# A linear-attention and feed-forward kernel: its small matmuls on four quarters of the TensorE array

## The chip, the cores and the metric

The program runs on one core of one Trainium2 chip, in one launch. The metric is the device time of the execution in microseconds; a profiled execution gives in addition the trace from which the rows below are taken.

## What is computed

Four batches of 768 tokens with 8 heads of 48 channels go through a gated linear attention, and its output through a feed-forward layer with an ELU:

```python
for t in range(S):
    state = alpha[:, :, t, :, None] * state + np.einsum('bhd,bhe->bhde', k[:, :, t], v[:, :, t])
    y[:, :, t] = np.einsum('bhd,bhde->bhe', q[:, :, t], state)
x = y.transpose(0, 2, 1, 3).reshape(3072, 384)
h = x @ w_in                              # 384 -> 2048
g = np.where(h > 0, h, np.exp(np.minimum(h, 0)) - 1)
out = g @ w_out                           # 2048 -> 384
```

All inputs and the output are float32.

## The kernel before

**Attention by windows.** The tokens are cut into 24 windows `i` of 128 tokens, six to a batch (`NW`), each of two chunks of 64 tokens. Heads go in pairs: `n` is the pair (0 to 3), `a` the head within it; on the 128 partitions head `a` has rows 64a to 64a + 47. Each piece of a window is a token of the program, a function of some lines:

- `L`, `LV`, `V0` (L155, L173, L180): loads of k, q, alpha (tile `qka`), of v (tile `vs`), and of a copy of v of which only the first 64 tokens are filled, the rest zero (tile `v0`).
- `SC` (L189): running product P of alpha. `LN`, `EX` (L198, L203): its inverse R. `KA`, `KB`, `KC` (L211, L216, L221): k scaled by it. `SQ` (L235): q scaled, into tile `st`; from window 6 on (`EARLY`) each head's half of `st` apart, and `ZS` (L242) clears the other half. `PC` (L225) sums P for a check of ranges.
- `TA`, `TB` (L266): scaled k transposed in blocks of 32 by 32 on VectorE, into tile `kn`, eight instructions each.
- `S` (L293): the scores of a chunk's 64 tokens among themselves; per chunk, pair and head one fp32 matmul of 64 weight columns and 64 moving columns, 16 a window. `MK` (L301): the mask, from PSUM into the other half of `st`.
- `U` (L315): what the window adds to the state, `kn` against v, 48 columns by 48; `x = 0` from the first 64 tokens (with `v0`), `x = 1` from all 128, 8 matmuls each; a batch's last window has `x = 0` only. Both lie in one PSUM bank, tile `u`. `UA`, `UB`, `UC` (L331, L333, L362, L364): the states from it.
- `Y` (L380): the output of the window, one matmul per chunk, pair and head, over state and scores at once (128 rows), 16 a window. `XH`, `XL`, `XD` (L433, L434, L456, L460, L467): it is split into an upper and a lower part and put into the layout of x.

In windows before `EARLY` the matmuls of S and U have other shapes: S has 48 rows, on the rows of its head, and writes to the same half of the partitions (tiles (0,0) and (1,1) of four of 64 by 64); U has weights 64 columns wide, with 128 rows for `x = 1` and 64 rows for `x = 0`. The early Y has two matmuls one after the other on the same tile, one for the state and one for the scores, for each chunk, pair and head.

**Feed-forward by blocks.** A block `b` has 256 tokens, and eight steps `j`. A step is `A` (L577): 18 matmuls of 128 by 128 by 256 columns into tile `h`; `RA`, `RB` on ScalarE (L585, L590), `RC` on VectorE (L595), `GH` on ScalarE (L601) and `GL` on VectorE (L614), which make the ELU and split it into `gh` and `gl`; and `O` (L628): 12 matmuls of 384 columns into the two banks of `o`. `Z` (L636, L639) stores a block. `CA`, `CB`, `LC` check ranges of the weights.

**What sets the order.** The list `START`, written out by hand, gives the order of the first part. From step n = 25 on (n = 8b + j) the function `steady` writes the order: each step has A(n), its five elementwise operations, and O of step n - 2; every window's tokens are put at fixed steps, one window in four steps. `at(n, start, names)` puts the tokens of window i at step 4i + start. Y of a window, U of the next and S of the one behind it stand in one step, ahead of its A. Each engine runs its instructions in this order. All PSUM tiles come from one pool of eight banks.

In the trace and below an fp32 matmul stands as two passes, each with a weight load; the matmuls of A and O are one pass each.

Of the kernel before, what the change touches and what calls it, by code (L numbers as in the profile page):

```python
# [8 lines left out]
F32 = mybir.dt.float32  # L9
# [55 lines left out]
GH.2.1 LV.11 SQ.9 ZS.9 RA.2.4 XL.7 RB.2.4 GL.2.2 UC.8 SC.10 XD.7 LN.10 EX.10 GL.2.1 S.9 PC.9 TA.9 KA.10 A.2.5  # L65
RA.2.5 O.2.1 RB.2.5 O.2.2 RC.2.4 A.3.0 UA.8 A.2.7 RC.2.5 GH.2.6 GH.2.4 RA.3.0 RB.3.0 O.2.3 MK.9 RA.2.7 S.8
GH.2.5 GL.2.4 O.2.4 TB.9 GL.2.6 GL.2.5 UB.6 RB.2.7 LV.9 V0.9 MK.8 L.11 KB.10 KC.10 SQ.10 ZS.10 RC.3.0 RC.2.7
O.2.5 GH.3.0 TB.10 TA.10 GL.3.0 GH.2.7 GL.2.7 V0.10 O.2.6
"""

@with_exitstack
def gla_elu_ffn(ctx: ExitStack, tc: tile.TileContext, qka, vv, vn, wgt, out):
    nc = tc.nc
# [7 lines left out]
    psa = main.enter_context(tc.tile_pool(name="psa", bufs=8, space=bass.MemoryType.PSUM))  # L81
# [55 lines left out]
    win = [{} for _ in range(NWIN)]  # L137
# [38 lines left out]

    @tok
    def V0(i):
        if i >= EARLY:
            nc.sync.dma_start(out=v0[i % 2][0:64], in_=vv[i, 0:64, HD:2 * HD])  # L180

    @tok
# [54 lines left out]

    @tok
    def ZS(i):
        if i >= EARLY:  # L240
            for a in range(2):
                nc.gpsimd.memset(win[i]["st"][64 - 64 * a:128 - 64 * a, a], 0.0)  # L242

# [54 lines left out]
    def MK(i):  # L298
        d = win[i]
        for o, a in ([(slice(0, 128), 1)] if i < EARLY else [(slice(64, 128), 0), (slice(0, 64), 1)]):  # L300
            nc.vector.tensor_tensor(  # L301
                out=d["st"][o, a].rearrange("p n (c t) -> p c n t", c=2), in0=d["sc"][o],
                in1=mask[o].unsqueeze(1).unsqueeze(1).broadcast_to([o.stop - o.start, 2, NP, C]), op=ALU.mult)

    @tok
    def U(i):
        d = win[i]
        u = d["u"] = psa.tile([128, 2, NP, D], F32, name="u", tag="pa")
        m = 64 if i < EARLY else D
        for x in ((1, 0) if i % NW < NW - 1 else (0,)):  # L310
            r = slice(0, C) if x == 0 and i < EARLY else slice(0, 128)
            v = d["vn"] if x or i < EARLY else v0[i % 2].rearrange("p (h e) -> p h e", e=D)
            for n in range(NP):
                for a in range(2):
                    nc.tensor.matmul(u[64 * a:64 * a + m, x, n, :], lhsT=d["kn"][r, n, a, 0:m],  # L315
                                     rhs=v[r, 2 * n + a, :],
                                     start=(x == int(i % NW < NW - 1) and n == 0), stop=True, skip_group_check=True)


    def rows(i):  # L320
        return [slice(0, 128)] if i < EARLY else [slice(0, D), slice(64, 64 + D)]

    def state(i, r, c):
        a = r.start // 64
        return lhs(i, c, a)[r, 0:NP * D].rearrange("p (n e) -> p n e", e=D)


    def diff(i, out, r, x):
        u = win[i]["u"][r, x]
        if i % NW == 0 or i in UPE:  # L330
            nc.scalar.mul(out=out, in_=u, mul=-1.0)  # L331
        else:
            nc.vector.tensor_tensor(out=out, in0=state(i, r, 0), in1=u, op=ALU.subtract)  # L333

    @tok
    def UP(i):
        for x in range(2 if i % NW < NW - 1 else 1):
            for a in range(2 if i >= EARLY else 1):
                r = slice(64 * a, 64 * a + D) if i >= EARLY else slice(0, 128)
                nc.tensor.matmul(win[i]["u"][r, x], lhsT=minus[:, r].bitcast(F32), rhs=lhs(i, 0, a)[:, 0:NP * D],  # L340
                                 start=False, stop=True, skip_group_check=True)

    @tok
    def UA(i):
        for r in rows(i):
# [328 lines left out]
    start = [t.split(".") for t in START.split()]  # L674
# [10 lines left out]
def steady(n0=25):  # L685


    p, late = [], [divmod(n, NJ) for n in range(n0 - 2, n0)]

    def at(n, start, names, end=NWIN):  # L690
        if (n - start) % 4 == 0 and (n - start) // 4 < end:
            p.extend((x, (n - start) // 4) for x in names)

    def second(b, j):
        p.append(("O", b, j))
        if j == NJ - 1:
            p.append(("Z", b))

    for n in range(n0, NBLK * NJ):
        b, j = divmod(n, NJ)  # L700
        at(n, -18, ("V0",))
        at(n, -22, ("L", "LV"))
        at(n, -7, ("Y",))
        at(n, -11, ("U",))
        at(n, -15, ("S",))
        if n == 4 * NWIN - 4:
            p.append(("VP",))
        p.extend((x, b, j) for x in ("A", "RA"))
        at(n, -17, ("LN",))
        p.append(("RB", b, j))  # L710
        at(n, -17, ("EX", "KA", "KB", "ZS", "ZV"))
# [12 lines left out]
        at(n, -7, ("XL", "XD"))
        at(n, -11, ("UA", "UB", "UC"))
        at(n, -13, ("MK",))
        at(n, -14, ("PC",))
# [188 lines left out]
```

## Time and profile before

| | us |
|---|---|
| median of 3 runs | 523.03 (522.64 to 526.26) |
| profiled execution | 524.14 |
| its span, first to last instruction | 522.4 |
| TensorE busy | 509.1 |
| VectorE busy | 396.4 |
| ScalarE busy | 298.0 |
| GpSimd busy | 133.0 |

The span is the time between the first and the last instruction in the trace; the profiled execution has some time around it. Busy time of an engine is the time in which at least one of its instructions runs. Matmuls are pipelined, so their rows overlap: how long one costs is read from the distance of starts, not from its duration.

### The profile page before, as it was taken

The page shows a single profiled execution, that of the slowest core. Times are in us where ns is not written, and L with a number is a line of the kernel's source. Part 1 is how long each engine was busy: PE and PEld are TensorE (multiplying, and loading weights), DVE is VectorE, ACT ScalarE, POOL GpSimd, SP SyncE. Part 2 cuts the span into 40 slices and gives each one's busy share as a digit, 9 for nine tenths or more (in the row PEclk, how much of TensorE's full clock was granted, in tenths as well). Part 3 has the DMA queues.
Part 4 walks back from the last instruction along what each step waited for, and adds up shares of the span by engine and source line. Part 5 has one row for each costly group of instructions (what it writes and reads, how often), then busy time and mean ns, then how long its engine had stood idle before and what let it go on. Part 6 is the DMA issues. An engine that isn't in the chain of part 4 may idle for free.

```text
span 522.4 us, 13159 instructions
## 1 busy us (share of the span) xinstructions
PE 509.1 (97%) x5398; PEld 490.4 (94%) x5406; DVE 396.4 (76%) x781; ACT 298.0 (57%) x682; POOL 133.0 (25%) x137
## 2 busy tenths in 40 slices
PE   6899999999999999999999999999999999999996
PEld 3688899999999999999999999999999999999996
DVE  7889999899998777776877887786887877334431
ACT  3337576455652657657656657557657656654442
POOL 2214552434230034044044044043043140000000
PEclk8889999999999999999999999999999999999999
DMA  8992930415122234344344254254154131110001
GB/s 301 412 375 55 414 118 1 159 54 189 66 77 69 84 115 137 100 130 136 89 141 137 74 157 137 62 167 136 57 174 136 36 101 42 48 52 9 30 3 35
DMA packets 23843, 62.90 MB, mean 120 GB/s; under 512 B 3168, under 2 KB 11232, under 8 KB 23776
## 3 DMA queue, kind: packets, MB, share of 16 engines
q1 hardware_dynamic: 23488, 61.60, 36.1%
q8 instruction: 44, 0.72, 0.6%
q10 hardware_dynamic: 288, 0.39, 0.2%
q14 instruction: 23, 0.19, 0.1%
HBM read 55.30 MB, written 4.72 MB: 115 GB/s over the span
## 4 chain that ended last, share of the span: by engine, by line
PE 96%; DVE 2%; DMA 1%; issue 1%; SPq 0%; ACT 0%; DVEq 0%
PE h L577 40%; PE o L628 39%; PE sc L293 5%; PE y L380 4%; PE u L315 3%; PE y L375 2%; DMA qka<-in_qka_dram 1%; PE tp L256 1%; PE wp L109 1%; PE y L419 1%; DVE st L232 0%; PE yl L375 0%; DVE wm L515 0%; DVE P L189 0%; SPq L159 0%
## 5 line engine op out<-in xcount | busy, mean ns | idle before, releaser
L577 PE MATMUL h<-xt,w 128*128 128x256 f32 x1728 | 222.5, 283 | 0.0
L577 PEld LDWEIGHTS h<-xt,w 128*128 128x128 f32 x1728 | 213.7, 188 | 2.0
L628 PE MATMUL o<-w,gh 128*128 128x384 f32 x768 | 198.6, 340 | 0.0
L628 PEld LDWEIGHTS o<-w,gh 128*128 128x128 f32 x768 | 135.6, 188 | 0.4
L628 PE MATMUL o<-w,gl 128*128 128x384 f32 x384 | 129.8, 338 | 0.0
L585 ACT ACTIVATE r<-h 128x512 f32<-128x512 f32 x96 | 57.4, 598 | 110.8 <-PE h L577 102.9
L595 DVE SCALAR_TENSOR_TENSOR h<-r,h 128x512 f32<-128x512 f32 x96 | 66.2, 694 | 66.8 <-ACT r L590 66.4
L601 ACT CAST gh<-h 128x512 fp32r<-128x512 f32 x96 | 56.0, 586 | 66.2 <-DVE h L595 54.9
L614 DVE TENSOR_TENSOR gl<-h,gh 128x512 fp32r<-128x512 f32 x96 | 65.7, 686 | 32.2 <-ACT gh L601 31.3
L266 DVE STREAM_TRANSPOSE kn<-qka 32x128 f32<-32x128 f32 x288 | 87.0, 302 | 3.8
L235 POOL TENSOR_TENSOR st<-qka,P 64x512 f32<-64x512 f32 x30 | 36.3, 1209 | 200.4 <-PE h L577 109.0
L628 PEld LDWEIGHTS o<-w,gl 128*128 128x128 f32 x384 | 72.2, 188 | 0.0
L590 ACT ACTIVATE r<-r 128x512 f32<-128x512 f32 x96 | 60.3, 631 | 2.2
L189 DVE TENSOR_TENSOR_SCAN P<-qka,first 128x516 f32<-128x516 f32 x24 | 30.5, 1274 | 2.4 <-DMA qka<-in_qka_dram 1.8
L211 POOL TENSOR_TENSOR qka<-qka,R 128x512 f32<-128x512 f32 x18 | 23.5, 1306 | 27.8 <-ACT R L203 20.8
L301 DVE TENSOR_TENSOR st<-sc,mask 64x512 f32<-64x512 f32 (+1 forms) x42 | 28.9, 688 | 1.9 <-PE sc L293 0.8
L216 POOL TENSOR_TENSOR R<-P,R 128x512 f32<-128x512 f32 x20 | 25.6, 1278 | 16.0 <-DVE qka L211 12.8
L293 PE MATMUL sc<-st,qka 128*64 128x64 f32 (+1 forms) x768 | 29.2, 232 | 0.0
L293 PEld LDWEIGHTS sc<-st,qka 128*64 128x64 f32 (+1 forms) x768 | 26.4, 146 | 2.2 <-issue 1.8
L380 PEld LDWEIGHTS y<-st,vs 128*64 128x64 f32 x576 | 18.2, 138 | 4.5 <-issue 4.3
L533 ACT ACTIVATE ck<-ck,lim 128x384 f32<-128x384 f32 x32 | 21.0, 655 | 1.0
L380 PE MATMUL y<-st,vs 128*64 128x64 f32 x576 | 20.7, 225 | 0.0
(87 smaller groups left out, 424.4 us busy)
## 6 DMA issues: line engine op xcount, KB each, us to landing
qka<-in_qka_dram SPq DMA_DIRECT2D x22, 770.0 KB, 5.6
raw<-in_wgt_dram SPq DMA_DIRECT2D x16, 768.0 KB, 11.4
ck<-in_wgt_dram SPq DMA_DIRECT2D x32, 384.0 KB, 3.5
vs<-in_vv_dram SPq DMA_DIRECT2D x36, 192.0 KB, 5.4
out_dram<-ot SPq DMA_DIRECT2D x22, 192.0 KB, 2.7
vs<-in_vv_dram SPq DMA_DIRECT2D x6, 384.0 KB, 10.2
xt<-y SPq DMA_DIRECT2D x40, 48.0 KB, 3.1
v<-in_vv_dram SPq DMA_DIRECT2D x18, 96.0 KB, 3.1
```

The lines of the kernel that those rows point to most:

```text
L189: nc.vector.tensor_tensor_scan(out=P.rearrange("p n w -> p (n w)"), data0=t[:, 2 * NP * W:], data1=first.rearrange("p n w -> p (n w)"), in ...
L235: eng(SQV, i).tensor_tensor(out=st[r, a], in0=d["q"][r], in1=pw(i)[r], op=ALU.mult)
L266: nc.vector.transpose(out=kn[32 * t:32 * t + 32, :, 32 * g:32 * g + 32], in_=d["kt"][32 * g:32 * g + 32, :, 32 * t:32 * t + 32])
L293: nc.tensor.matmul(sc[o, c, n, :], lhsT=d["kt"][r, n, cs], rhs=d["st"][r, 0 if i < EARLY else a, n, cs], start=(c == 0 and n == 0), stop=T ...
L380: nc.tensor.matmul(out[64 * a:64 * a + m], lhsT=lhs(i, c, a)[:, n * D:n * D + m], rhs=d["st"][:, a, n, c * C:(c + 1) * C], start=start, st ...
L577: nc.tensor.matmul(h[:, f, :], lhsT=t[:, wi, ws], rhs=x[:, c, xi, :], start=(f == 0 and k == 0), stop=(k == 8), skip_group_check=True)
L585: nc.scalar.activation(out=r, in_=d["h"], func=AF.Relu, scale=-1.0)
L590: nc.scalar.activation(out=d["r"], in_=d["r"], func=AF.Exp, scale=-1.0)
L595: nc.vector.scalar_tensor_tensor(out=d["h"], in0=d["r"], scalar=-1.0, in1=d["h"], op0=ALU.add, op1=ALU.max)
L601: nc.scalar.copy(out=gh, in_=d["h"])
L614: nc.vector.tensor_tensor(out=gl, in0=d["h"], in1=d["gh"].bitcast(F32), op=ALU.subtract)
L628: nc.tensor.matmul(o[:, 0:DM], lhsT=gt[:, f, ms], rhs=t[:, wi, f * DM:f * DM + DM], start=(j == 0 and f == 0 and k == 0), stop=(j == NJ - ...
```

## The change

From window 10 on (`QUAD`) U has another form, from window 11 on S has.

- **U4** replaces the two halves of U, all tokens and first 64 tokens, by the first and the second 64 tokens: `x` is the half of the tokens, and with it the 64 rows of the array; `a` is the head, and with it the 64 columns. A matmul has 64 rows, 64 weight columns (all of `kn`'s, with padding) and 48 moving columns. Each half x has a PSUM bank of its own (tiles `q`). A batch's last window has x = 0 only.
- **S4** has for each head `a` and chunk `c` the 48 rows of the head and writes to the partitions of the chunk. The scores lie behind U's columns in the two banks that U4 of the window before got, by head.
- Both loops run over `QUADS`, so that four matmuls that follow each other are on four quarters of the array.
- `MK` becomes four operations of 64 x 256, in two parts. `UB` starts from what `UA` made, since u's second part is now of the second tokens alone, and is there in a batch's first window too; `UC` has one form.
- `V0` ends with window 9, `ZS` with window 10.
- `steady` puts tokens at other places: XH, XL, XD ahead of A; SC ahead of RA; LN and EX behind GH and one step earlier; KA and KB one step earlier; KC at the end of its step, also one earlier; the transposes in pieces (T.0 and T.1, T.2, T.3) over three steps instead of one; MK in two pieces; UA ahead of GH; PC one step later. The check of the weights moves by two steps.

```diff
+    QUADS = ((0, 0), (1, 1), (0, 1), (1, 0))
+    def S4(i):
+        d = win[i]
+        d["s4"] = [t[:, NP * D:NP * (D + C)].rearrange("p (n t) -> p n t", n=NP) for t in win[i - 1]["q4"]]
+        for n in range(NP):
+            for a, c in QUADS:
+                r, cs = slice(64 * a, 64 * a + D), slice(c * C, (c + 1) * C)
+                nc.tensor.matmul(d["s4"][a][64 * c:64 * c + 64, n, :], lhsT=d["kt"][r, n, cs], rhs=d["st"][r, a, n, cs],
+                                 start=(n == 0 and a == 1 and i % NW == 0), stop=True, skip_group_check=True)
...
+        if i > QUAD:
+            for a, c in QUADS[2 * part:2 * part + 2] if part < 2 else QUADS:
+                o, r = slice(64 * c, 64 * c + 64), slice(64 - 64 * a, 128 - 64 * a)
+                nc.vector.tensor_tensor(
+                    out=d["st"][r, a, :, c * C:(c + 1) * C], in0=d["s4"][a][o],
+                    in1=mask[o].unsqueeze(1).broadcast_to([64, NP, C]), op=ALU.mult)
+            return
...
+    def U4(i):
+        d = win[i]
+        d["q4"] = banks(i)
+        d["u"] = [t[:, 0:NP * D].rearrange("p (n e) -> p n e", n=NP) for t in d["q4"]]
+        for n in range(NP):
+            for x, a in QUADS if i % NW < NW - 1 else QUADS[::2]:
+                r = slice(64 * x, 64 * x + 64)
+                nc.tensor.matmul(d["u"][x][64 * a:64 * a + 64, n, :], lhsT=d["kn"][r, n, a, :],
+                                 rhs=d["vn"][r, 2 * n + a, :], start=(n == 0), stop=True, skip_group_check=True)
...
-        if i >= EARLY:
+        if EARLY <= i < QUAD:
             nc.sync.dma_start(out=v0[i % 2][0:64], in_=vv[i, 0:64, HD:2 * HD])
...
-        at(n, -16, ("TA", "TB"))
...
+        at(n, -14, "T.2")
+        at(n, -13, "MK.1", "PC")
+        at(n, -13, "T.3")
+        at(n, -17, "KC")
+        at(n, -16, "T.0", "T.1")
```

TensorE, a step of the steady part with a window in it, before (`o`: O's tiles, `y`, `u`, `sc`: those of Y, U and S, `h`: A's):

```order
L628 MATMUL o<-w_756,gh 128x384 x2
L628 MATMUL o<-w_756,gl 128x384
L380 MATMUL y<-st,vs_106 64x64 x16
L315 MATMUL u<-vs_107,kn 48x48 x8
L315 MATMUL u<-v_113,kn 48x48 x8
L293 MATMUL sc<-st,qka 64x64 x16
L577 MATMUL h<-xt,w_909 128x256 x18
```

and such a step of the changed kernel (`q`: the shared banks):

```order
L675 MATMUL o<-w_756,gl 128x384
L427 MATMUL y<-st,vs_108 64x64 x16
L345 MATMUL q<-vs_105,kn 64x48 x16
L302 MATMUL q<-st,qka 64x64 x16
L624 MATMUL h<-xt,w_909 128x256 x18
L675 MATMUL o<-w_756,gh 128x384 x2
```

The place and the number of matmuls are the same; the outputs of U are 64 partitions and no longer 48, and S and U write the same tiles.

VectorE in the steady part, before, from RC and GL (`h`, `gl`) of the step ahead of MK (`st<-sc`) to those of the step behind the transposes (`kn`):

```order
L595 SCALAR_TENSOR_TENSOR h<-r,h 128x512
L614 TENSOR_TENSOR gl<-h,gh 128x512
L301 TENSOR_TENSOR st<-sc,mask 64x2x4x64 x2
L595 SCALAR_TENSOR_TENSOR h<-r,h 128x512
L221 SCALAR_TENSOR_TENSOR qka<-R,qka 128x512
L614 TENSOR_TENSOR gl<-h,gh 128x512
L266 STREAM_TRANSPOSE kn<-qka 32x4x32 x16
L595 SCALAR_TENSOR_TENSOR h<-r,h 128x512
L614 TENSOR_TENSOR gl<-h,gh 128x512
```

and the same stretch of the changed kernel:

```order
L269 STREAM_TRANSPOSE kn<-qka 32x4x32 x4
L642 SCALAR_TENSOR_TENSOR h<-r,h 128x512
L329 TENSOR_TENSOR st<-q,mask 64x4x64 x2
L661 TENSOR_TENSOR gl<-h,gh 128x512
L329 TENSOR_TENSOR st<-q,mask 64x4x64 x2
L269 STREAM_TRANSPOSE kn<-qka 32x4x32 x4
L224 SCALAR_TENSOR_TENSOR qka<-R,qka 128x512
L642 SCALAR_TENSOR_TENSOR h<-r,h 128x512
L661 TENSOR_TENSOR gl<-h,gh 128x512
L269 STREAM_TRANSPOSE kn<-qka 32x4x32 x8
```

The sixteen transposes that stood in one run are now three runs in three steps, the masks stand on both sides of a GL, and KC (`qka<-R,qka`) has gone from ahead of a GL to the end of the step before.

## Rows read from the trace of the kernel before

**Rows 1.** The page: span, TensorE's busy time, the chain that ended last by engine.

```profile
span 522.4 us, 13159 instructions
...
PE 509.1 (97%) x5398; PEld 490.4 (94%) x5406; DVE 396.4 (76%) x781; ACT 298.0 (57%) x682; POOL 133.0 (25%) x137
...
PE 96%; DVE 2%; DMA 1%; issue 1%; SPq 0%; ACT 0%; DVEq 0%
```

**Rows 2.** Busy time by stretch (instructions), then clock, DMA: one of twelve, and their sum.

```profile
300.00:320.00 20.00, 20.00 (x218) 19.68 (x218) 16.47 (x37) 12.37 (x31) 5.90 (x6) 1.00 0.45 130
...
sum 240.00, PE 240.00 PEld 236.14 DVE 189.39 ACT 151.98 POOL 71.78; mean PE 20.00 PEld 19.68 DVE 15.78 ACT 12.66 POOL 5.98
```

**Rows 3.** Timeline, TensorE, a full window's step: start, length, engine, line, shapes, count.

```profile
307.26 1.15 PE L380 MATMUL y<-st,vs 128*64 128x64 f32 x32
308.24 0.53 PE L315 MATMUL u<-vs,kn 128*48 128x48 f32 x16
308.60 0.53 PE L315 MATMUL u<-v,kn 128*48 128x48 f32 x16
308.96 1.12 PE L293 MATMUL sc<-st,qka 128*64 128x64 f32 x32
310.00 2.38 PE L577 MATMUL h<-xt,w 128*128 128x256 f32 x18
312.22 0.52 PE L628 MATMUL o<-w,gh 128*128 128x384 f32 x2
...
314.34 2.30 PE L577 MATMUL h<-xt,w 128*128 128x256 f32 x18
316.48 0.52 PE L628 MATMUL o<-w,gh 128*128 128x384 f32 x2
```

**Rows 4.** Timelines of TensorE up to chosen moments: the small matmuls of some windows.

```profile
308.96 0.23 PE L293 MATMUL sc<-st,qka 128*64 128x64 f32 x1
...
308.96 0.24 PE L293 MATMUL sc<-st,qka 128*64 128x64 f32 x2
...
72.69 0.91 PE L293 MATMUL sc<-st,qka 48*64 48x64 f32 x24
...
72.69 1.15 PE L293 MATMUL sc<-st,qka 48*64 48x64 f32 x32
...
90.94 0.61 PE L315 MATMUL u<-vs,kn 64*64 64x48 f32 x14
...
90.94 0.67 PE L315 MATMUL u<-vs,kn 64*64 64x48 f32 x16
...
40.38 1.27 PE L315 MATMUL u<-vs,kn 128*64 128x48 f32 x32
...
98.11 2.13 PE L375 MATMUL y<-st,vs 48*64 48x64 f32 x64
```

**Rows 5.** Timeline, TensorE, as in rows 3: last windows of batches.

```profile
208.80 0.53 PE L315 MATMUL u<-v,kn 128*48 128x48 f32 x16
...
210.20 2.38 PE L577 MATMUL h<-xt,w 128*128 128x256 f32 x18
...
447.60 0.53 PE L315 MATMUL u<-v,kn 128*48 128x48 f32 x16
448.06 2.38 PE L577 MATMUL h<-xt,w 128*128 128x256 f32 x18
```

**Rows 6.** VectorE's groups, 200 to 430 us: count, busy us, mean ns, idle ahead.

```profile
L266 DVE STREAM_TRANSPOSE kn<-qka 32x128 f32<-32x128 f32 x183 | 55.3, 302 | 2.3
L595 DVE SCALAR_TENSOR_TENSOR h<-r,h 128x512 f32<-128x512 f32 x47 | 32.7, 696 | 26.0 <-ACT r L590 25.8
...
L301 DVE TENSOR_TENSOR st<-sc,mask 64x512 f32<-64x512 f32 x24 | 16.5, 689 | 0.7
...
L221 DVE SCALAR_TENSOR_TENSOR qka<-R,qka 128x512 f32<-128x512 f32 x12 | 8.2, 684 | 0.0
L333 DVE TENSOR_TENSOR vs<-vs,u 48x192 f32<-48x192 f32 x18 | 6.2, 347 | 0.1
```

More of the change, by code (lines that the diff above doesn't have):

```diff
@@ L32 @@
 WARM = 12
+QUAD = 10
 WLV, KAV, KBV, SQV = (0, 1, 2, 7, 9, 11, 15), (0, 1, 3, 4, 5, 9), (0, 1, 4, 7), (0, 1, 2, 6, 7, 10)
@@ L67 @@
 GH.2.5 GL.2.4 O.2.4 TB.9 GL.2.6 GL.2.5 UB.6 RB.2.7 LV.9 V0.9 MK.8 L.11 KB.10 KC.10 SQ.10 ZS.10 RC.3.0 RC.2.7
-O.2.5 GH.3.0 TB.10 TA.10 GL.3.0 GH.2.7 GL.2.7 V0.10 O.2.6
+O.2.5 GH.3.0 TB.10 TA.10 GL.3.0 GH.2.7 GL.2.7 O.2.6
 """
@@ L239, in ZS @@
     def ZS(i):
-        if i >= EARLY:
+        if EARLY <= i <= QUAD:
             for a in range(2):
@@ L269, in TA, with T @@
     @tok
+    def T(i, g):
+        blocks(i, (g,))
+    @tok
     def TA(i):
@@ L281, in KN, with banks @@
         nc.scalar.copy(out=kn, in_=d["tp"].rearrange("p n (a x) -> p n a x", a=2))
+    def banks(i):
+        return [psa.tile([128, 512], F32, name="q", tag="pa") for _ in range(2)]
+    QUADS = ((0, 0), (1, 1), (0, 1), (1, 0))
[7 more added lines that the diff above has]
+                                 start=(n == 0 and a == 1 and i % NW == 0), stop=True, skip_group_check=True)
     @tok
@@ L285, in S @@
         d = win[i]
+        if i > QUAD:
+            return S4(i)
         sc = d["sc"] = psa.tile([128, 2, NP, C], F32, name="sc", tag="pa")
@@ L297, in MK @@
     @tok
-    def MK(i):
+    def MK(i, part=2):
         d = win[i]
+        if i <= QUAD and part == 0:
+            return
+        if i > QUAD:
+            for a, c in QUADS[2 * part:2 * part + 2] if part < 2 else QUADS:
[3 more added lines that the diff above has]
+                    in1=mask[o].unsqueeze(1).broadcast_to([64, NP, C]), op=ALU.mult)
+            return
         for o, a in ([(slice(0, 128), 1)] if i < EARLY else [(slice(64, 128), 0), (slice(0, 64), 1)]):
@@ L307, in U @@
         d = win[i]
-        u = d["u"] = psa.tile([128, 2, NP, D], F32, name="u", tag="pa")
+        if i >= QUAD:
+            return U4(i)
+        u = psa.tile([128, 2, NP, D], F32, name="u", tag="pa")
+        d["u"] = [u[:, 0], u[:, 1]]
         m = 64 if i < EARLY else D
@@ L314, in U @@
                 for a in range(2):
-                    nc.tensor.matmul(u[64 * a:64 * a + m, x, n, :], lhsT=d["kn"][r, n, a, 0:m],
+                    nc.tensor.matmul(d["u"][x][64 * a:64 * a + m, n, :], lhsT=d["kn"][r, n, a, 0:m],
                                      rhs=v[r, 2 * n + a, :],
@@ L328, in diff @@
     def diff(i, out, r, x):
-        u = win[i]["u"][r, x]
-        if i % NW == 0 or i in UPE:
+        u = win[i]["u"][x][r]
+        half = i >= QUAD and x == 1
+        if (i % NW == 0 or i in UPE) and not half:
             nc.scalar.mul(out=out, in_=u, mul=-1.0)
         else:
-            nc.vector.tensor_tensor(out=out, in0=state(i, r, 0), in1=u, op=ALU.subtract)
+            nc.vector.tensor_tensor(out=out, in0=state(i, r, int(half)), in1=u, op=ALU.subtract)
     @tok
@@ L339, in UP @@
                 r = slice(64 * a, 64 * a + D) if i >= EARLY else slice(0, 128)
-                nc.tensor.matmul(win[i]["u"][r, x], lhsT=minus[:, r].bitcast(F32), rhs=lhs(i, 0, a)[:, 0:NP * D],
+                nc.tensor.matmul(win[i]["u"][x][r], lhsT=minus[:, r].bitcast(F32), rhs=lhs(i, 0, a)[:, 0:NP * D],
                                  start=False, stop=True, skip_group_check=True)
@@ L350, in UB @@
     def UB(i):
-        if i % NW < NW - 1 and i % NW and i not in UPE:
+        if i % NW < NW - 1 and (i >= QUAD or i % NW and i not in UPE):
             for r in rows(i):
-                diff(i, win[i]["u"][r, 1], r, 1)
+                diff(i, win[i]["u"][1][r], r, 1)
     @tok
@@ L360, in UC @@
             for r in rows(i + 1):
-                if i % NW and i not in UPE:
-                    nc.vector.tensor_tensor(out=state(i + 1, r, 0), in0=d["u"][r, 1], in1=pe[r], op=ALU.mult)
+                if i >= QUAD or i % NW and i not in UPE:
+                    nc.vector.tensor_tensor(out=state(i + 1, r, 0), in0=d["u"][1][r], in1=pe[r], op=ALU.mult)
                 else:
-                    nc.vector.scalar_tensor_tensor(out=state(i + 1, r, 0), in0=d["u"][r, 1], scalar=-1.0,
+                    nc.vector.scalar_tensor_tensor(out=state(i + 1, r, 0), in0=d["u"][1][r], scalar=-1.0,
                                                    in1=pe[r], op0=ALU.mult, op1=ALU.mult)
@@ L685, in steady, with at @@
 def steady(n0=25):
+    LEFT = dict(T=11)
     p, late = [], [divmod(n, NJ) for n in range(n0 - 2, n0)]
-    def at(n, start, names, end=NWIN):
-        if (n - start) % 4 == 0 and (n - start) // 4 < end:
-            p.extend((x, (n - start) // 4) for x in names)
+    def at(n, start, *names):
+        i, r = divmod(n - start, 4)
+        if r == 0 and LEFT.get(names[0].split(".")[0], 0) <= i < NWIN:
+            for x in names:
+                x, *k = x.split(".")
+                p.append((x, i, *map(int, k)))
     def second(b, j):
@@ L700, in steady @@
         b, j = divmod(n, NJ)
[L701 to L705, printed above, removed]
+        at(n, -22, "L", "LV")
+        at(n, -7, "Y")
+        at(n, -11, "U")
+        at(n, -15, "S")
         if n == 4 * NWIN - 4:
             p.append(("VP",))
[L708 to L711, printed above, removed]
+        at(n, -7, "XH", "XL", "XD")
+        p.append(("A", b, j))
+        at(n, -18, "SC")
+        p.extend((x, b, j) for x in ("RA", "RB"))
         p.append(("RC", b, j))
-        at(n, -16, ("KC",))
-        at(n, -18, ("SC", "SQ"))
+        at(n, -18, "SQ")
+        at(n, -11, "UA")
+        at(n, -13, "MK.0")
         p.append(("GH", b, j))
-        at(n, -7, ("XH",))
-        for start, h in ((21, 0), (24, 1)):
+        at(n, -18, "LN", "EX", "KA", "KB", "ZV")
+        for start, h in ((23, 0), (24, 1)):
             h += (n - start) // 4 * 2
@@ L722, in steady @@
         p.append(("GL", b, j))
-        at(n, -16, ("TA", "TB"))
[L724 to L727, printed above, removed]
+        at(n, -11, "UB", "UC")
+        at(n, -14, "T.2")
[3 more added lines that the diff above has]
+        at(n, -16, "T.0", "T.1")
         if n == 4 * NWIN - 7:
```

## The prediction

> **What bounds the kernel now.** The first view to read is the page's head: of a span of 522.4 us TensorE is busy 509.1, and the chain of work that ended last is 96% TensorE [rows 1]. A busy TensorE need not be a full one, so the second view is the busy time by stretch: over twelve stretches of 20 us from 200 to 440 us TensorE has 240.00 of 240.00, VectorE 189.39, ScalarE 151.98 and GpSimd 71.78, at a granted clock of 1.00, which is the 2.4 GHz level [rows 2]. The third view is TensorE's timeline over one step with a window in it [rows 3]: 12 matmuls of O end, then 32 passes of Y, 32 of U and 32 of S start one behind the other, then the 18 of A, and no row names a releaser. From the starts: Y takes 308.24 - 307.26 = 0.98 us, U 0.36 + 0.36, S 1.04, A 2.22. So in the steady part a microsecond taken from TensorE's own work is a microsecond of the span, as long as nobody becomes late. (An fp32 matmul of the program is two passes, two records, in the trace.)
>
> **How the passes lie.** Two passes of S start together, within 0.01 us: the first alone has a row of 0.23 us, both together one of 0.24 [rows 4]. They are the two column halves of the array (heads a = 0 and 1). The next pair comes a weight load later: 24 passes that ran up to one moment span 0.91 us, all 32 span 1.15, so four pairs cost 0.24, **0.06 a pair**. For U with weights 64 wide and 48 moving columns 14 passes span 0.61 and 16 span 0.67, again 0.06 [rows 4]; with weights 48 wide, as U has now, 16 passes take 0.36, 0.045 a pair [rows 3]. So the width of the weights sets the round of a tile, and two tiles share a round. That the halves run as queues of their own is seen in the early Y at 98.11: there two matmuls, four passes, stand in a row for the same tile before the other tile's four. Were they started strictly in order, four passes would cost three rounds and a bit, about 0.19 us; 64 passes span 2.13, so about (2.13 - 0.24)/63 = 0.030 each, 0.12 for four [rows 4]. The engine does look past passes that wait for their tile.
>
> **The change, part by part.** What matters is that S and U now use four tiles of 64 by 64, in the order (0,0), (1,1), (0,1), (1,0). The number of matmuls stays: 16 of S, 16 of U (8 in a batch's last window). If four tiles share a round as two do, 32 passes are 8 rounds of 0.06 = 0.48 us.
>
> U4 and S4 stand together in 13 steps (U of windows 10 to 22, S of 11 to 23), and U of window 23 alone in one. Windows 11, 17 and 23 are last windows.
> - Before, a full step has U + S = 310.00 - 308.24 = 1.76 us [rows 3]; a step with a last window's U has 210.20 - 208.80 = 1.40; U of window 23 with the way to A 448.06 - 447.60 = 0.46 [rows 5].
> - After: U4 8 rounds, 0.48. The weights are now the whole 64 columns, so the round is 0.06 and not 0.045. A last window's U4 has only tokens' half 0, two tiles: 16 passes, 8 rounds, 0.48 too, where it had 0.36.
> - S4 0.48, and what S has beyond its rounds stays: 1.04 - 16 x 0.06 = 0.08.
> - Y keeps 128 rows, U4 has 64, so the array changes its shape between them, which it did not before. The early U changes from 128 to 64 rows in its middle: its 32 passes span 1.27 where S of the same width without that change spans 1.15 [rows 4]. I take 0.12. Bounds: nothing, and 0.19, which is what leaving S costs now (A takes 2.22 behind S, 312.22 - 310.00, and 2.14 behind O, 316.48 - 314.34 [rows 3]: 0.08, and not more than 0.11 at S's end).
>
> Sum: a full step 1.76 - (0.48 + 0.48 + 0.08 + 0.12) = 0.60, eleven times 6.60; a last window's step 1.40 - 1.16 = 0.24, twice 0.48; window 23's U 0.46 - (0.48 + 0.10 + 0.12) = -0.24. **Together 6.84 us.** With r for the round of four tiles the sum is 18.36 - 192 r: 16 rounds in each of eleven steps and S's 8 in two.
>
> What costs nothing, and under what cover:
> - **Masks.** MK is four operations of 64 x 256 for two of 64 x 512 at 0.689 us. Between the 192-column row (0.347) and that one [rows 6] a 256-column one lies at about 0.43: 4 x 0.43 - 1.38 = +0.34 us per window on VectorE; the bounds, 0.35 and 0.69, make it 0 to 1.4. UB in windows 12 and 18 adds two operations of about 0.35.
> - **New order on VectorE.** The 16 transposes (0.302 each, 4.8 us in a run) are split 8 + 4 + 4 over three steps. The fullest step is then RC and GL (0.70 each), four masks 1.72, four transposes 1.21, KC 0.68: 5.0 us against a TensorE step of 2.12 + 2.14 = 4.26 [rows 3, 6]. The step behind has RC, GL and eight transposes, 3.8; the one with Y lasts over 6 us on TensorE. GL(n) is wanted by O(n), which stands behind A(n+2): two steps of 4.26 from A(n)'s end to that place, against 3.5 or so for RA, RB, RC, GH and GL. So 0.7 us of lateness is covered, about 5 us are. Cover gone, it would cost 0.7 in each of 13 windows.
> - **SC** goes ahead of RA to RC in its step: 1.2 us on VectorE, behind which RC and GL queue. Its input is loaded four steps earlier.
> - **XH, XL and XD** go ahead of A. XH waits for Y; behind it on ScalarE is RA, which needs A, 1.2 us of U and S and 2.2 of A later. XD's DMAs leave SP earlier.
> - **GpSimd** loses two memsets a window, SP one DMA; neither is waited for here.
> - **Two shared banks** are held from U(i) to MK(i+1), two steps, where before one bank was held so long and one for a step. Y, U4 and A take theirs over from h tiles whose GL was waited for by an O already passed, so no new stall.
>
> **A rule against the change.** The smallest mean spacing that any row shows is U's 0.36/16 = 0.0225 us a pass [rows 3]; pairs start closer, but never pair after pair. S4 and U4 want 0.06/4 = 0.015. The Trainium skill, "TensorEngine Tiling (Array Packing)", section Instruction Overhead, says that a matmul has some 60 cycles of overhead and that no tiling factor should be taken from a dimension that is already small; here 48 and 64 columns move. At 2.4 GHz that would be 25 ns a pass, r = 0.10 and a loss of 0.8 us, an estimate from that page. By that rule U's passes could not come at 0.0225; the trace has them below it.
>
> **Rivals.**
> 1. *Four tiles share the round, stretched.* If each further tile adds up to its start offset, r = 0.06 + 2 x 0.01 = 0.08: gain 3.0, 520.0 us. For it: four tiles have more weights and columns to fetch in a round than two, and no row shows that. Against it: the early S on 48 rows and the S on 128 have the same round, so what is fetched did not set it [rows 3, 4].
> 2. *The issue is the limit*, at U's 0.0225 a pass, r = 0.09: gain 1.1, 521.9 us. For it: nothing faster is in the trace. Against it: U's round fits the width of its weights (0.045 at 48, 0.06 at 64), so U is not limited by issue. This is what the page's rule above would do here.
> 3. *Two at a time; it becomes slower.* Tiles (0,0) and (1,0) write the same half of PSUM's partitions, into two banks, and no row of before has two row groups at once on one column group: the early S has only the diagonal. If they take turns, r = 0.12 and the sum is 18.36 - 23.04 = -4.7, 527.7 us. It decides from r = 18.36/192 = 0.096 on.
> 4. *VectorE late.* The 0.7 us of its fullest step reaches O each time: 13 x 0.7 = 9 us lost, 525.3 us. Against it: VectorE has 189.39 of 240 [rows 2], about 83% after, and two steps of slack.
>
> **The numbers.** The profiled execution is 524.14 us, 1.74 around its span of 522.4; the median of the runs is 523.03. The sum makes the span 515.6; I put it against the median: 523.03 - 6.84 = **516.2 us**. Chances: as forecast (r up to 0.064, shape change up to 0.19: 515 to 517.5) 0.62; stretched 0.15; issue 0.11; two at a time 0.07; VectorE late 0.05. Low end: the shape change costs nothing, 14 x 0.12 = 1.7 more, 514.5. High end takes in rivals 1 and 2: 522.0. About 1% (5.2 us) is what a measurement here tells from no change. Faster by over 1% is the forecast case but for its slow edge, 0.59; within 1% takes that edge, rivals 1, 2 and most of 3 and 4, 0.37; slower 0.04.
>
> **What would show it.** In the steady part U4 and S4 follow Y with 32 passes of about 0.48 us each, four starts close together in every 0.06; about 0.1 us between Y and U4; A behind S4 still 2.22; O 2.12; U + S with A's start 1.16 after Y. Wrong would be: rounds of 0.09 or 0.12; a gap before U4 over 0.2; idle time of weight loads before O released by GL or GH; any wait for a bank. If steps without a window are longer than 4.26 us, VectorE or ScalarE is late, and my cover was not there.

## The result, and the profile after

The changed kernel takes 517.33 us (median of 6 runs, 514.8 to 519.26) against 523.40 for the kernel before, run beside it (6 runs, 522.64 to 526.38). The ratio is 0.9866, with a 95% interval of 0.9828 to 0.9905. The profiled execution took 517.54 us, its span is 515.8. Forecast were 516.2, and 515.6 for the span.

The page of the changed kernel: its span, the busy time of the engines, the chain that ended last by engine. It answers [rows 1].

```profile
span 515.8 us, 13180 instructions
PE 502.3 (97%) x5406; PEld 481.6 (93%) x5406; DVE 402.3 (78%) x811; ACT 300.2 (58%) x682; POOL 119.5 (23%) x111
PE 94%; DVE 3%; DMA 1%; issue 0%; SPq 0%; ACT 0%; DVEq 0%
```

TensorE is busy 6.8 us less (509.1 before) and still all that counts. By stretch, one row and the sum of the twelve from 200 to 440 us, as in [rows 2]: TensorE is full in all of them, at the 2.4 GHz level, and VectorE has gone from 189.39 to 199.17.

```profile
300.00:320.00 20.00, 20.00 (x223) 19.61 (x222) 17.11 (x40) 12.77 (x32) 5.43 (x7) 1.00 0.34 105
sum 240.00, PE 240.00 PEld 235.08 DVE 199.17 ACT 156.74 POOL 57.33; mean PE 20.00 PEld 19.59 DVE 16.60 ACT 13.06 POOL 4.78
```

The timeline of TensorE over a full window's step, which answers [rows 3]:

```profile
225.91 1.15 PE L427 MATMUL y<-st,vs 128*64 128x64 f32 x32
226.99 0.68 PE L345 MATMUL q<-vs,kn 64*64 64x48 f32 x32
227.49 0.66 PE L302 MATMUL q<-st,qka 48*64 48x64 f32 x32
228.08 2.41 PE L624 MATMUL h<-xt,w 128*128 128x256 f32 x18
230.33 0.52 PE L675 MATMUL o<-w,gh 128*128 128x384 f32 x2
...
232.44 2.30 PE L624 MATMUL h<-xt,w 128*128 128x256 f32 x18
234.58 0.52 PE L675 MATMUL o<-w,gh 128*128 128x384 f32 x2
```

From the starts: Y 1.08 us (0.98 before), U4 0.50 (0.72), S4 0.59 (1.04), A behind them 2.25 (2.22), O 2.11, A behind O 2.14. Y, U, S and A together take 4.42 where they took 4.96, a gain of 0.54 per full step. The last window's U is behind Y by 1.08 here too, and then (tiles `q` of U4 and S4, and the U4 of window 23 alone):

```profile
207.59 0.60 PE L345 MATMUL q<-vs,kn 64*64 64x48 f32 x13
...
208.67 1.46 PE L624 MATMUL h<-xt,w 128*128 128x256 f32 x10
...
440.52 0.67 PE L345 MATMUL q<-vs,kn 64*64 64x48 f32 x16
441.12 1.10 PE L624 MATMUL h<-xt,w 128*128 128x256 f32 x7
```

U4 and S4 take 1.08 there (1.40 before), and U4 alone 0.60 (0.46), each with 0.10 more for Y: gains of 0.2, and a loss of 0.24.

**The measure used below.** The start and the end of the program differ by some us from one execution to the next, in stretches that these kernels share. So each run is also read from the start of Y in step 25 to the check of the weights near the end (tile `vd`), which holds all steps that the change touches. The two ends in the kernel before:

```profile
167.93 1.15 PE L380 MATMUL y<-st,vs 128*64 128x64 f32 x32
...
496.32 0.19 PE L669 MATMUL vd<-one,okp 128*1 128x1 f32 x2
```

and in the changed one:

```profile
167.16 1.15 PE L427 MATMUL y<-st,vs 128*64 128x64 f32 x32
...
489.41 0.19 PE L716 MATMUL vd<-one,okp 128*1 128x1 f32 x2
```

328.39 and 322.25: the stretch is 6.14 us shorter. The eleven full steps, two last windows and window 23 give 11 x 0.54 + 2 x 0.2 - 0.24 = 6.1. All of the gain is there.

| kernel | the stretch, us | against the changed kernel | median of the run, ratio to before [95%] |
|---|---|---|---|
| before | 328.39 | +6.14 | |
| changed | 322.25 | | 517.33, 0.9866 [0.9828, 0.9905] |
| e1 new order alone | 328.39 | +6.14 | 522.78, 0.9988 [0.9966, 1.0010] |
| e2 new matmuls alone | 322.44 | +0.2 | 515.84, 0.9858 [0.9828, 0.9887] |
| e3 two tiles after two | 326.66 | +4.4 | 522.12, 0.9959 [0.9931, 0.9987] |
| e4 U4 with weights 48 wide | 320.75 | -1.5 | 514.25, 0.9829 [0.9792, 0.9866] |
| e5 Y between U4 and S4 | 323.90 | +1.65 | 518.95, 0.9905 [0.9878, 0.9932] |
| e7 small matmuls added | 327.52 | +5.3 | 521.84, 0.9977 [0.9955, 1.0000] |
| e9 T.3 three times | 350.59 | +28.3 | 546.41, 1.0425 [1.0368, 1.0483] |
| e10 T.3 twice | 329.48 | +7.2 | 523.66, 1.0013 [0.9984, 1.0042] |
| e11 T.1 three times | 341.64 | +19.4 | 536.12, 1.0254 [1.0216, 1.0292] |
| e12 as much as e10, in the gaps | 322.25 | 0.0 | 516.52, 0.9874 [0.9831, 0.9918] |

(e5 is read from the start of its first small matmul in step 25, U at 164.32, since Y stands behind U there.)

### The profile page after: what moved, and what is told of

It reads as the page before. It is cut to its first block, busy times and chain, and to the rows that moved or that the text cites. A ratio compares the mean times of both kernels' runs of the same rounds, so it can differ in the third digit from the quotient of the medians.

```text
span 515.8 us, 13180 instructions
## 1 busy us (share of the span) xinstructions
PE 502.3 (97%) x5406; PEld 481.6 (93%) x5406; DVE 402.3 (78%) x811; ACT 300.2 (58%) x682; POOL 119.5 (23%) x111
## 4 chain that ended last, share of the span: by engine, by line
PE 94%; DVE 3%; DMA 1%; issue 0%; SPq 0%; ACT 0%; DVEq 0%
PE h L624 41%; PE o L675 40%; PE y L427 4%; PE sc L317 2%; PE q L345 2%; PE u L361 1%; PE y L422 1%; PE q L302 1%; DMA qka<-in_qka_dram 1%; PE wp L112 1%; PE tp L259 1%; DVE st L235 0%; DVE P L192 0%; DVE spare L556 0%; DVE wm L562 0%; PE y L466 0%
## 5 line engine op out<-in xcount | busy, mean ns | idle before, releaser
L642 DVE SCALAR_TENSOR_TENSOR h<-r,h 128x512 f32<-128x512 f32 x96 | 66.2, 693 | 54.1 <-ACT r L637 53.5
L648 ACT CAST gh<-h 128x512 fp32r<-128x512 f32 x96 | 56.1, 587 | 83.8 <-DVE h L642 73.0
L661 DVE TENSOR_TENSOR gl<-h,gh 128x512 fp32r<-128x512 f32 x96 | 66.1, 690 | 32.0 <-ACT gh L648 31.3
L637 ACT ACTIVATE r<-r 128x512 f32<-128x512 f32 x96 | 60.4, 632 | 2.6
L219 POOL TENSOR_TENSOR R<-P,R 128x512 f32<-128x512 f32 x20 | 25.6, 1280 | 15.8 <-DVE qka L214 12.7
L329 DVE TENSOR_TENSOR st<-q,mask 64x256 f32<-64x256 f32 x52 | 22.0, 422 | 1.0
L201 ACT ACTIVATE R<-P 128x512 f32<-128x512 f32 x24 | 15.2, 633 | 8.2 <-DVE P L192 8.2
L575 ACT ACTIVATE ck<-ck 128x384 f32<-128x384 f32 x32 | 18.2, 569 | 1.8 <-DMA ck<-in_wgt_dram 1.7
```

Source lines behind the costliest of these rows:

```text
L219: eng(KBV, i).tensor_tensor(out=d["R"], in0=pw(i), in1=d["R"], op=ALU.mult)
L637: nc.scalar.activation(out=d["r"], in_=d["r"], func=AF.Exp, scale=-1.0)
L642: nc.vector.scalar_tensor_tensor(out=d["h"], in0=d["r"], scalar=-1.0, in1=d["h"], op0=ALU.add, op1=ALU.max)
L648: nc.scalar.copy(out=gh, in_=d["h"])
L661: nc.vector.tensor_tensor(out=gl, in0=d["h"], in1=d["gh"].bitcast(F32), op=ALU.subtract)
```

## The experiments

### Order or matmuls

The theory: the gain is that of the array alone. The rival: the new order has a share in it, or is needed for it. e1 keeps the new order and lets U and S have their old forms to the end (with V0 and ZS, which these need):

```diff
-QUAD = 10
+QUAD = 24
```

> The changed kernel with U and S in their old form in every window (QUAD = 24, v0 loaded and the score tiles cleared again); of the change only the new order of steps is left. Theory (the gain is TensorE's own time in U4 and S4, and TensorE waited for nobody before): U 0.72, S 1.04, A 2.22, steps without a window 4.26 as before, and the time is that of the kernel before, 523.4 us within 1 us. Rival (the new order is what gains): 517 to 518 us with U and S as slow as before.

The stretch is that of the kernel before, 328.39, to the last hundredth, and the run is not to be told from it. e2 has the new U4, S4 and masks in the old order of `steady` (the transposes in one run five steps ahead of U, MK in one piece, XH to XD behind A):

```diff
-        at(n, -13, "MK.0")
...
-        at(n, -14, "T.2")
-        at(n, -13, "MK.1", "PC")
-        at(n, -13, "T.3")
-        at(n, -17, "KC")
-        at(n, -16, "T.0", "T.1")
+        at(n, -16, ("TA", "TB"))
+        at(n, -13, ("MK",))
+        at(n, -16, ("KC",))
```

> The changed kernel with the old table of steps: all sixteen transposes in one run of 4.8 us, four masks in one place, KC ahead of a GL. Theory (VectorE has two steps of cover, also in the old order): U4 0.50 and S4 0.59 as in the changed kernel, no idle of TensorE, 517.3 us within 1 us. Rival (the new order is needed, because the shorter steps and the 0.3 us more of masks make GL late): idle time of TensorE ahead of O or A in each window, 0.3 us or more in 13 windows, 521 us or more.

322.44, within 0.2 of the changed kernel. The median of its runs, 515.84, lies 0.5 us below the band that I had given, a difference that the stretch does not show. One wait that the changed kernel has not is of that size (columns: who waited for whom, us, times, longest us; PEld is TensorE's weight load):

```profile
PEld h L624 <- ACT r L637: 0.3, 1, 0.3
```

So the matmuls carry the whole gain, and the new order neither gives nor is needed for it.

### Are four tiles more than two

If the four quarters gave nothing over the two of the diagonal, nothing would be lost by running all matmuls of (0,0) and (1,1) first, and then those of (0,1) and (1,0). e3 does that in both loops:

```diff
-        for n in range(NP):
-            for a, c in QUADS:
+        for n, (a, c) in [(n, q) for p in (QUADS[:2], QUADS[2:]) for n in range(NP) for q in p]:
```

> The changed kernel with the same matmuls of U4 and S4 in another order: first all on tiles (0,0) and (1,1), then all on (0,1) and (1,0), so that only two of four tiles find work in the queue at a time. Theory (four queues that share a round of 0.058 us): 16 rounds instead of 8, U4 and S4 0.47 us longer each in 13 steps, U of the three last windows one tile at a time and 0.47 longer too, which is in that count, and U of window 23 0.47: 12.7 us in all, 530 us. Rival (the gain comes from 64 rows instead of 128, or from the order of steps, not from four at a time): 517 to 518 us.

It loses 4.4 us in the stretch: neither the doubled rounds that I had forecast (12.7) nor the nothing of the rival. The timeline shows why (U4 is L344, S4 L301, A L623):

```profile
228.15 0.77 PE L344 MATMUL q<-vs,kn 64*64 64x48 f32 x26
228.71 0.27 PE L301 MATMUL q<-st,qka 48*64 48x64 f32 x2
228.76 0.28 PE L344 MATMUL q<-vs,kn 64*64 64x48 f32 x3
...
229.62 2.38 PE L623 MATMUL h<-xt,w 128*128 128x256 f32 x18
```

S4's first passes start at 228.71 while U4's last are still to come at 228.76 and later: passes of two instruction groups, on other tiles, go past one another. U4 and S4 take 1.47 us here and 1.09 in the changed kernel, not the 1.9 of 32 rounds of 0.059. So the engine itself went past waiting passes and filled part of the other two quarters; by handing it four quarters in turn, the change gets the rest. In rounds of two tiles the new shape alone would gain nothing: 1.9 us is no less than the 1.76 of the old U and S.

### What sets the round

Rivals 1 and 2 were about the size of a round. The theory says that the weight width of a tile sets it, as with two tiles; then U4 with 48 weight columns must be faster again. e4 leaves `kn`'s padding out:

```diff
-                nc.tensor.matmul(d["u"][x][64 * a:64 * a + 64, n, :], lhsT=d["kn"][r, n, a, :],
+                nc.tensor.matmul(d["u"][x][64 * a:64 * a + D, n, :], lhsT=d["kn"][r, n, a, 0:D],
```

> The changed kernel with U4's weights 48 columns wide instead of 64 (the padding is not loaded). Theory (the width of the weights sets the round, also with four tiles): round 0.045 instead of 0.058, 8 rounds, U4 0.40 instead of 0.50 us, in 14 steps 1.5 us, 515.8 us. Rival (four tiles are at the limit of issue with 0.0146 us a pass): U4 stays at 0.50 and the time at 517.3 us.

```profile
225.97 0.57 PE L345 MATMUL q<-vs,kn 64*48 64x48 f32 x32
226.37 0.66 PE L302 MATMUL q<-st,qka 48*64 48x64 f32 x32
```

U4 takes 0.40 us where it took 0.50, so a round is 0.10/8 shorter, 0.046; the stretch is 1.5 us shorter. By its median, 514.25 us, this is the fastest version found; its interval overlaps that of the changed kernel, and the stretch is the clearer sign. e7 asks how small a round can be: per full window 16 matmuls more, with 32 weight columns and 32 moving columns, whose results nobody reads.

```diff
+        for n in range(NP):
+            for x, a in QUADS if i % NW < NW - 1 else ():
+                r = slice(64 * x, 64 * x + 64)
+                nc.tensor.matmul(d["q4"][x][64 * a:64 * a + 32, 448:480], lhsT=d["kn"][r, n, a, 0:32],
+                                 rhs=d["vn"][r, 2 * n + a, 0:32], start=False, stop=True, skip_group_check=True)
```

> The changed kernel with sixteen more matmuls behind U4 in each of eleven windows, on the four tiles with weights of 32 columns and 32 moving columns, into unused columns of the banks; nothing reads them. Theory (a round is the width of the weights over 1.2 a ns and 5 ns more, also at four tiles): 8 rounds of 0.032, 0.25 us a window, 2.8 us in all in the steady part. Rival (issue limits at the 0.0123 us a pass that U4 with 48 columns has): 0.39 us a window, 4.3 us; at 0.0146: 0.47 and 5.1 us.

```profile
226.42 0.68 PE L345 MATMUL q<-vs,kn 64*64 64x48 f32 x32
227.03 0.45 PE L350 MATMUL q<-vs,kn 64*32 64x32 f32 x32
227.42 0.69 PE L302 MATMUL q<-st,qka 48*64 48x64 f32 x32
```

The added 32 passes fill 0.39 us, 0.012 each with what leaves and enters their shape; of those that had started by 227.20:

```profile
227.03 0.36 PE L350 MATMUL q<-vs,kn 64*32 64x32 f32 x20
```

The other twelve passes, three rounds, add 0.09 (0.45 for all 32), so a round is 0.03 us and a pass 0.0075. The rival's limit of issue, 0.0123 or 0.0146 us a pass, is not there. The total fits neither side as forecast: the stretch grew by 5.3 us, 0.48 a window, where the theory had 2.8 us (0.25 a window), and the rival's 5.1 comes near it by another way. The rest stands where the array changes its shape, from 64 weight columns to 32 and back: U4 takes 0.61 there (0.50 before), the addition 0.15 more than its rounds, S4 0.62 (0.59 before), and the A behind is 0.03 shorter. That the change of shape is what these cost is argued from their place, and from e5 below. Since the moving columns went down to 32 with the weights, e7 cannot say which of the two sets the 0.03; e4, where 48 columns move as in U4, can.

### The change of shape

Y has 128 rows, U4 has 64. e5 puts Y between U4 and S4, so that the array changes to 64 rows, to 128 and back to 64 in each step:

```diff
-        at(n, -7, "Y")
         at(n, -11, "U")
+        at(n, -7, "Y")
         at(n, -15, "S")
```

> The changed kernel with Y between U4 and S4 instead of ahead of both: the same matmuls, but the array goes from 64 to 128 rows and back once more in each of 13 steps. Theory (a change of shape costs what the early U shows, 0.12 to 0.14 us): each of these steps 0.13 us longer, the steady part from the Y of step 25 to the last check 1.5 to 2 us longer than the changed kernel's 322.24. Rival (the shape change is free, and Y's longer step comes from the wait for banks): 322.2 us again.

```profile
223.25 0.68 PE L345 MATMUL q<-vs,kn 64*64 64x48 f32 x32
223.86 1.15 PE L427 MATMUL y<-st,vs 128*64 128x64 f32 x32
224.95 0.69 PE L302 MATMUL q<-st,qka 48*64 48x64 f32 x32
225.57 2.40 PE L624 MATMUL h<-xt,w 128*128 128x256 f32 x18
```

From U4 to A 2.32 us, where the changed kernel has 2.17; the stretch 1.65 us longer, 13 x 0.13. One more change between small matmuls of unlike shape costs 0.13 to 0.15 us here; the prediction had 0.12.

### How near VectorE is

Rival 4 had VectorE late. Before the result I gave it 0.05, with a cover (the time by which a result is there before it is wanted) of 5 us from GL to O. e9 repeats the last run of transposes, +2.4 us of VectorE in each window, with the same inputs and outputs:

```diff
-        at(n, -13, "T.3")
+        at(n, -13, "T.3", "T.3", "T.3")
```

> The changed kernel with the last four transposes of each window done three times over: 2.4 us more of VectorE in the fullest of its four steps, 13 windows. Theory (GL has two steps of cover, about 5 us, and VectorE has 16.6 of 20 us to do): VectorE is late by about 3 us in that step, has caught up when Y's step ends, and TensorE is not held up: the steady part stays at 322.2 us within 0.5. Rival (what VectorE is late reaches O): up to 3 us in each of 13 windows, 340 us or more.

My theory expected no change, and fell: 28.3 us are lost. TensorE waits inside U4, for `kn`. VectorE's transposes, and TensorE's rows:

```profile
226.59 4.00 DVE L269 STREAM_TRANSPOSE kn<-qka 32x128 f32<-32x128 f32 x12
...
229.47 0.31 PE L345 MATMUL q<-vs,kn 64*64 64x48 f32 x2
230.70 0.68 PE L345 MATMUL q<-vs,kn 64*64 64x48 f32 x30 [0.91 <-issue]
```

The transposes end at 230.59, and U4 goes on at 230.70; its row names no releaser (`issue`), so that it waited for them is read from these times. Not all of the loss is waiting: behind four of these waits the granted clock fell for some us. In the stretch

```profile
260.00:280.00 20.00, 18.43 (x196) 17.83 (x195) 16.87 (x42) 11.50 (x28) 4.87 (x4) 0.91 0.42 122
```

it was 0.50, the 1.2 GHz level, from 276 to 278, after TensorE had stood idle for 1.56 us up to 273.68, and the A that ran then took 3.61 us from its start to O's, where it takes 2.25 otherwise. In e11 below this came twice, in e10 not at all.

So O was not the first to suffer. In the changed kernel the last transposes,

```profile
224.10 1.26 DVE L269 STREAM_TRANSPOSE kn<-qka 32x128 f32<-32x128 f32 x4
```

end at 225.36, and U4 starts at 226.99: the thin cover is 1.6 us there. (KC, right behind them, ends at 226.09, and S4, which needs it, starts at 227.49. That cover is 1.4 us, as thin; S4 stands behind U4, and waited for KC only in last windows, 0.6 us in e10.) From that came a second theory, that only running over this cover costs; against it stood a third, that VectorE's amount of work counts wherever it lies. e10 adds half as much, which fits into 1.6 us; e11 adds as much as e9, but five steps ahead of U4.

```diff
-        at(n, -13, "T.3")
+        at(n, -13, "T.3", "T.3")
```

> The four transposes of T.3 stand twice in the order of every window, with the same inputs and outputs: 4 x 0.30 = 1.2 us more of VectorE just ahead of the place where U4 needs them. In the changed kernel T.3 ends 1.6 us before U4 starts. Theory (the thin cover is that of T.3 to U4, 1.6 us, and the loss with T.3 three times came from running over it): 1.2 us fit, the stretch from Y of step 25 to the last check matmul stays 322.2 us (within 0.4), no wait of TensorE in it. Rival (VectorE's work as such is what counts): half of the loss of T.3 three times, 322.2 + 14 = 336 us.

```diff
-        at(n, -16, "T.0", "T.1")
+        at(n, -16, "T.0", "T.1", "T.1", "T.1")
```

> The four transposes of T.1 stand three times in the order of every window, same inputs and outputs: 8 x 0.30 = 2.4 us more of VectorE per window, as much as with T.3 three times, but at the end of a step that lies five steps ahead of the window's U4. Behind them stand RC, GL, T.2 and the masks of later steps. Theory (place, not amount): U4 has several steps of cover there and O some 5 us, so the stretch from Y of step 25 to the last check matmul stays 322.2 us (within 0.5). Rival (amount: VectorE is full and any 2.4 us a window are paid): 350.6 us, as with T.3 three times.

Both theories missed. e10 lost 7.2 (not 0, and not 14), e11 19.4 (not 0, and not 28). In e10 the first U4s did not wait; then lateness had built up, and eight did, such as this one:

```profile
265.68 0.31 PE L345 MATMUL q<-vs,kn 64*64 64x48 f32 x2
266.28 0.68 PE L345 MATMUL q<-vs,kn 64*64 64x48 f32 x30 [0.28 <-issue]
```

VectorE went round in a time of its own. One of its RC, and the same four steps later:

```profile
240.18 0.70 DVE L642 SCALAR_TENSOR_TENSOR h<-r,h 128x512 f32<-128x512 f32 x1 [0.46 <-ACT r L637]
...
260.34 0.70 DVE L642 SCALAR_TENSOR_TENSOR h<-r,h 128x512 f32<-128x512 f32 x1 [0.47 <-ACT r L637]
```

They lie 20.16 us apart; in the changed kernel four steps take 19.41. What that is made of stands in VectorE's timeline of the changed kernel, over one such round (L642 RC, L661 GL, L648 GH and L637 RB on ScalarE):

```profile
264.89 0.69 DVE L642 SCALAR_TENSOR_TENSOR h<-r,h 128x512 f32<-128x512 f32 x1
266.23 0.69 DVE L661 TENSOR_TENSOR gl<-h,gh 128x512 fp32r<-128x512 f32 x1 [0.65 <-ACT gh L648]
...
270.65 0.70 DVE L642 SCALAR_TENSOR_TENSOR h<-r,h 128x512 f32<-128x512 f32 x1 [0.54 <-ACT r L637]
...
276.78 0.69 DVE L661 TENSOR_TENSOR gl<-h,gh 128x512 fp32r<-128x512 f32 x1 [0.66 <-ACT gh L648]
...
279.21 0.70 DVE L642 SCALAR_TENSOR_TENSOR h<-r,h 128x512 f32<-128x512 f32 x1 [0.47 <-ACT r L637]
...
284.30 0.69 DVE L642 SCALAR_TENSOR_TENSOR h<-r,h 128x512 f32<-128x512 f32 x1
```

Between 264.89 and 284.30, 19.41 us, VectorE waits four times, 2.32 us, so it has 17.1 us to do. The two waits before GL come whenever RC and GL stand next to each other: RC ends, ScalarE does GH, and only then can GL start. They take 1.31 us however late VectorE is. The wait of 0.47 lies behind ScalarE's own run of GH, LN, EX, RA and RB, and I count it with them, 1.78 in all; the wait of 0.54 is for an A, and goes first when VectorE is late. So a round of VectorE is 17.1 + 1.8 = 18.9, half a us under TensorE's 19.4. With 1.2 more it is 20.1 (20.2 measured in e10), and with 2.4 more 21.3. In e9 it was 21.5, from the KC at 252.11 to the KC at 273.61, and 22.3 or so where the clock had fallen. This was worked out after these three runs; e12 tests it. It adds the same 1.2 us as e10, but two transposes each into the two gaps between RC and GL:

```diff
+        at(n, -16, "TX.0")
+        at(n, -14, "TX.2")
         p.append(("GL", b, j))
```

(`TX` is the first half of `T`, done once more.)

> Again 1.2 us more of VectorE per window (four transposes repeated, same inputs and outputs), but two of them between RC and GL in each of two steps of a window. There VectorE stands idle for 0.65 us in the changed kernel, since GL waits for GH on ScalarE and GH for RC. Theory (VectorE goes round in 17.06 us of work plus about 1.77 us a window in which it can only wait for ScalarE; with 1.2 us more at T.3 that is 20.0, over TensorE's 19.4): here the additions take the place of 1.2 us of that waiting, the round stays 18.8, below 19.4; the stretch from Y of step 25 to the last check matmul stays 322.2 us (within 0.6) and U4 does not wait. Rival (the amount of VectorE's work counts, wherever it stands): 329.5 us, as with T.3 twice.

The stretch is 322.25, that of the changed kernel. VectorE's waits from 200 to 440 us show where the added work went. The changed kernel:

```profile
DVE gl L661 <- ACT gh L648: 17.0, 26, 0.7
DVE h L642 <- ACT r L637: 16.6, 28, 1.1
```

e10, where the waits for GH stayed and only those for RB shrank:

```profile
DVE gl L661 <- ACT gh L648: 17.0, 26, 0.7
DVE h L642 <- ACT r L637: 7.7, 15, 0.9
```

e12, where the waits for GH are all but gone:

```profile
DVE h L652 <- ACT r L647: 16.1, 28, 1.1
DVE gl L671 <- ACT gh L658: 1.3, 2, 0.7
```

With 212.17 of 240 us busy in e12 (206.57 in e10) VectorE does more in the faster of the two. So neither the amount of work nor one cover decides, but whether the round, with the waits that cannot be worked off, stays under TensorE's. That the wait of 0.47 is one of these, the two rows of e10 above show: it comes back in each late round, as it does in e9 (0.47 at 266.41) and in e11 (0.47 at 243.30), while the one of 0.54 is gone. e11's round is 21.4 us (KC at 247.76 and at 269.21), so its transposes cost the round as much as e9's; it lost less in all because its first U4 to wait stands at 245.98 (208.55 in e9), and the clock fell twice and not four times.

## Why the prediction was right, point by point

- **What bounds the kernel.** Right: TensorE full at one clock level before and after, so its own time was the span's.
- **The round.** The term on which most hung was 0.06 us for four tiles. Eight rounds in a row: up to two moments, the changed kernel's U4 reads

```profile
226.99 0.27 PE L345 MATMUL q<-vs,kn 64*64 64x48 f32 x4
...
226.99 0.32 PE L345 MATMUL q<-vs,kn 64*64 64x48 f32 x6
```

  Four passes start within 0.02 us and span 0.27; the next come a round later. All 32 span 0.68, so a round is (0.68 - 0.27)/7 = 0.059.
- **The change of shape.** 0.12 forecast between Y and U4; it is 0.10 in Y's row and 0.03 in U4's (0.50 - 0.47), 0.13. S4 has 0.12 beyond its eight rounds (0.59 - 0.47), where I had kept 0.08, and A behind it 0.03 more; the sixteen rounds came 0.02 shorter. Together these are the 0.06 by which a full step gained less, 0.54 for 0.60, and 11 x 0.06 = 0.7 us of the sum: 6.14 for 6.84. That the profiled execution came within 0.3 us of 524.14 - 6.84 = 517.3 is partly the start and the end of the program, in which it was 0.5 us quicker than the profiled execution before.
- **Last windows.** Forecast +0.24 and -0.24, measured +0.2 and -0.24.
- **Masks.** 0.43 each forecast, 0.42 measured:

```profile
L329 DVE TENSOR_TENSOR st<-q,mask 64x256 f32<-64x256 f32 x48 | 20.3, 422 | 0.9
```

- **What costs nothing.** Right in the outcome: from 187 to 450 us no matmul waits. But the cover that I named was not the thin one. I set 0.7 us of lateness against 5 us from GL to O; e9 to e12 show that T.3 to U4 (1.6 us) is reached first, and that VectorE's round has half a us to spare. The fullest step of VectorE, forecast 5.0, is 5.1 (279.21 to 284.30). Before the change VectorE waited longer for RB, 26.0 us from 200 to 440 against 16.6 now, and about as long for GH (16.3, now 17.0): the change used up part of what was spare, on masks and by shorter steps.

**The rivals.** *Stretched round* (0.08): refuted, 0.059; the third and the fourth tile start within the same 0.02 us and cost nothing in the round. *Issue limit* (0.0225 a pass): refuted by U4's 0.0147 a pass and by the 0.0075 of e7; the rule of the Trainium skill, "TensorEngine Tiling (Array Packing)", section Instruction Overhead, of some 60 cycles a matmul, 25 ns at 2.4 GHz and a round of 0.10 (not this rival's 0.09) as an estimate, does not hold for these passes on separate tiles, and in e7 not even for a whole matmul of two passes, 15 ns. *Two at a time*: refuted; tiles that write the same half of PSUM's partitions into two banks share a round. *VectorE late*: it did not come, but its chance was nearer than 0.05 makes it look: 1.2 us more a window at T.3 take all of the gain, 7.2 for 6.14. The Trainium skill, "TensorEngine Tiling (Array Packing)", section PSUM Bottleneck, warns that copying out of PSUM may become the bottleneck when tiling makes TensorE faster; the trace points that way without reaching it, with VectorE's round of 18.9 against 19.4, in which the masks read PSUM but the transposes do not.

## What to carry to other kernels

Small matmuls on a part of the array were paid here by rounds that get longer with the width of a tile's weights, and tiles on unlike quarters shared them: hand the engine all quarters in turn, keep the weights no wider than they need be, and keep like shapes together, since a change of shape cost about two rounds. An engine that shows 86% busy can be full (VectorE in e10) and at 88% have room (e12): count with its work the waits that return whatever it does, and put new work into these. Before calling a cover large, look for the shortest one on the same engine, since a late engine is late everywhere. When long waits turn up on TensorE, look at the granted clock behind them before the loss is put down to the waits alone.

## What the hardware showed that was not expected

- With weights of 64, 48 and 32 columns four tiles had rounds of about 0.059, 0.046 and 0.03 us. From 64 to 48 only the weights changed (48 columns moved in both); at 32 the moving columns went down too, so there the width of the weights is not shown to be what sets it.
- Passes of different matmuls start out of the program's order when their tiles are free, across two groups of instructions (e3: S4 at 228.71, U4 still at 228.76).
- Between shapes of small matmuls (128 rows to 64, 64 weight columns to 32) lay 0.1 to 0.15 us, more than a round of four tiles (0.059).
- Behind six of the longer waits in U4 and S4 (four in e9, two in e11) the granted clock fell to its 1.2 GHz level for a few us, and an A took 3.6 to 3.8 us, where 2.25 is usual.
